# Sparse attention ahead of two dense layers: two tile groups per unit in place of three, a new order of steps, shorter lags and two early products

## The chip, the cores and the metric

The kernel runs on one core of one Trainium2 chip. The metric is the device time of one execution in microseconds (us). Engines are named as in the profile: PE is TensorE's matmul and PEld its weight load, DVE is VectorE, ACT is ScalarE, POOL is GpSimd, SP is SyncE, which issues the DMAs here.

## What is computed

```python
def _attn_ref(q, k, v):                       # B, H, S, D = 4, 8, 576, 64
    scores = scale * np.matmul(q, k.transpose(0, 1, 3, 2))
    mask_local = (rel >= 0) & (rel < 32)                     # heads 0 to 3
    mask_strided = (rel >= 0) & (pos[None, :] % 32 == pos[:, None] % 32)   # heads 4 to 7
    scores = np.where(masks, scores, -1e9)
    attn = softmax(scores)
    return np.matmul(attn, v)
...
x = attn_out.transpose(0, 2, 1, 3).reshape(2304, 512)
h = x @ w_in;  x = (h * np.cos(h)) @ w_out                   # 512 -> 2048 -> 512
g = x @ w_gate;  x = (g * sigmoid(g) * (x @ w_val)) @ w_out2   # 512 -> 1536 -> 512
```

The dense layers' weights come as 64-bit numbers in memory and are converted on the chip.

## The kernel before, in words

Attention works on 16 units (a batch and a pair of heads). Eight are local, with 9 tiles of 64 queries against 96 keys, and eight are strided, with 11 subtiles of 54 positions. Units go in pairs, one strided beside one local. `groups` (L78) cuts a unit into three groups: 3, 3 and 3 local tiles, or 4, 4 and 3 strided ones. The list `gs` (L780) has 48 groups, strided and local by turns, and the loop at L818 makes one step for each group and eight more to drain.

A group passes through several engines, one stage at a time, and `LAGS` says how many steps after its scores each stage is issued:

- `scores` (L460): PE multiplies q by k for each tile and head in 32-bit floats, into one PSUM bank. One matmul from `hot` (L472) fills the bank's columns that the tiles leave over, and one (L473) adds the mask. Together these two always cover 512 columns or nearly so.
- `top` (L475): DVE takes the row maxima of all the group's tiles in one instruction (L478).
- `exps` (L480), one step later: ACT, one instruction per tile (L484), into a buffer `e_l` or `e_s`.
- `sums` and `norm`, two steps later: DVE's row sums (L493) and reciprocals (L496), and POOL's multiplication (L498).
- `transposes` (L500), 5 steps later: PE. `evac` (L510): ACT copies the result out of PSUM (L515).
- `values` (L517), 6 steps later: PE multiplies by v (L526). `put` (L530), 7 steps later: ACT writes the result into `xy`, the dense layers' input.

All queues are filled in program order, with no scheduler, so an instruction that waits holds back everything behind it on its engine. Beside the groups, each step from number `KP` on calls `pump`, which takes work from a list `fill` until `PUMP` credits are spent. Here the list holds the preparation of `w_in`: for each of its 16 slices a maximum (L257) and two DVE steps of conversion (L261, L265), later a scaled high half on ACT (L275) and its low half on DVE (L278, called a lo here). Beside these stand maxima of the slices of `w_out` (L204, a scan here). One credit stands for about one microsecond of DVE.

The weight slices arrive through six buffers `raw`, each 512 KB: a scan or a conversion frees one and issues the next load. Loads of `w_out` are held back until step `RELEASE`.

After the last group's scores the loop drains. It starts the first of the dense layer's products there: `up1` (L604) for slice m = 0 is 12 matmuls of 512 columns, issued in two halves, `EARLY` being the number of such products. In other steps without scores `keep_warm` (L814) issues one small matmul. Then come 5 blocks of tokens with 16 slots each: a slot is one `up1`, a chain of ACT and DVE steps on its result (L617, L620, L624, L627), and pumped work. In block 0 the slots hold no second-layer matmuls. An `up1` needs a PSUM buffer: one of four `bank` tiles, or in some odd slots of block 0 an `acc` tile. A `bank` comes free when L627 has read it.

Of the kernel before, what the change touches and what calls it, by code (L numbers as in the profile page):

```python
# [20 lines left out]
STRIDE = 32  # L21
# [29 lines left out]
LAGS = (2, 5, 6, 7)  # L51
WARM = 11
PUMP, KP = 1.05, 8
XSAT = 12
EARLY, K0 = 1, 1
# [4 lines left out]
RELEASE = 30  # L60
# [17 lines left out]
def groups(p):  # L78
    return [(0, 3), (3, 3), (6, 3)] if is_local(p) else [(0, 4), (4, 4), (8, 3)]


def build(tc, qk_l, qk_s, v_l, v_s, w_in, w_out, w_gate, w_val, w_out2, fixed, out):
    nc = tc.nc
    wide = w_in.dtype != F32
    with ExitStack() as ctx:
# [322 lines left out]
        words = [128, 2 * LW, 2 * SW]  # L408
        fix = ap.tile([128, sum(words)], F32, name="fix", bufs=1)
        id32, ml, ms = (fix[:, sum(words[:i]):sum(words[:i + 1])] for i in range(3))  # L410
        ml, ms = (t.bitcast(BF16).rearrange("p (n w) -> p n w", n=4) for t in (ml, ms))
        e_s = [ap.tile([128, 2, 64, 2], F32, name=f"e_s{i}", bufs=1) for i in range(4)]
        e_l = [ap.tile([128, 3, LW + 1], F32, name=f"e_l{i}", bufs=1) for i in range(4)]
# [38 lines left out]
        class Group:  # L452
# [7 lines left out]
            def scores(self):  # L460
# [3 lines left out]
                mask = (ml[:, 0:3] if self.g == 0 else ml[:, 1:4]) if self.loc else ms[:, 0:n]  # L464
# [7 lines left out]
                nc.tensor.matmul(out=b[:, 288:512], lhsT=ones16, rhs=hot[:, 0:224], start=False, stop=False)  # L472
                nc.tensor.matmul(out=self.sc, lhsT=id16, rhs=mask, start=False, stop=True)  # L473

            def top(self):  # L475
                self.mx = ap.tile([128, 4], F32, name="mx", bufs=3)
                m = self.mx[:, 0:self.n]
                nc.vector.tensor_reduce(out=m, in_=self.sc, op=ALU.max, axis=AX.X, negate=True)  # L478

            def exps(self):  # L480
                self.t = (e_l if self.loc else e_s)[(self.i // 2 * 3 + self.g) % 4]
# [4 lines left out]
            def sums(self):  # L486

                self.ls = ap.tile([128, 4], F32, name="ls", bufs=5)
                if self.loc:
                    self.l, self.e = self.ls[:, 0:3], self.t  # L490
# [9 lines left out]
            def transposes(self):  # L500
                if self.loc:
                    self.tp = pa.tile([128, self.n, 128], F32, name="tp")[0:LW]
                    for i in range(self.n):
                        nc.tensor.transpose(self.tp[:, i, :], self.t[:, i, 0:LW], id32)
                else:
                    self.tp = pa.tile([128, 2, 128], F32, name="tp")
                    for i in range(2):
                        nc.tensor.transpose(self.tp[:, i, :], self.t[:, i].rearrange("p k u -> p (k u)"), id32)

            def evac(self):  # L510
                if self.loc:
                    self.pt = ap.tile([LW, 3, 128], F32, name="pt", bufs=2)
                else:
                    self.pt = ap.tile([128, 2, 128], F32, name="pts", bufs=2)
# [857 lines left out]
```

## Time and profile before

| | |
|---|---|
| median of 3 runs | 860.14 us (859.79 to 863.77) |
| the profiled execution: time, and its span | 859.9 us, 858.0 us |
| busy share of the span | PE 98%, PEld 70%, DVE 76%, ACT 61%, POOL 23% |
| last scores of attention, first unbroken run of dense matmuls | about 91 us, 101.8 us |
| granted TensorE clock | 0.999 of full speed |

Matmuls are pipelined, so a PE that counts as busy need not be at its peak; the distance from one start to the next tells what an instruction costs its engine. The last 750 us are dense products that PE streams almost without a break.

### The profile page before, as it was taken

The numbers are of one execution on the slowest core, as the hardware profiler recorded it, in microseconds if no ns is written. First come the engines' busy times: TensorE is split into PE (matmuls) and PEld (weight loads), VectorE is DVE, ScalarE is ACT, GpSimd is POOL, SyncE is SP. The second block draws the span as 40 slices with busy tenths as digits, with TensorE's granted clock in tenths as the row PEclk, the third lists the DMA queues.
The fourth block names the chain that finished last, engine by engine and source line by source line (L and its number), as shares of the span: only waits on it lengthen the run. The fifth ranks groups of instructions, "written<-read, shape, count | busy, mean of one in ns | idle before, by whom it ended". The sixth has DMA issues, their size and how long they took to land.

```text
span 858.0 us, 18371 instructions
## 1 busy us (share of the span) xinstructions
PE 844.6 (98%) x7223; PEld 601.7 (70%) x7223; DVE 653.0 (76%) x1256; ACT 519.4 (61%) x1047; POOL 197.8 (23%) x249
## 2 busy tenths in 40 slices
PE   9999999999999999999999999999999999999998
PEld 5776544444444444555666788888888899999998
DVE  6999989997888978788996378567756765765562
ACT  6898889554657766768885466545344444444440
POOL 4444234211445546423223100000000000000000
PEclk9999999999999999999999999999999999999999
DMA  9998832897567566515356257667776788789894
GB/s 364 408 359 283 276 105 74 278 343 261 165 201 244 193 215 205 177 34 179 129 194 249 71 196 282 230 217 261 239 261 232 244 274 288 277 310 321 321 321 143
DMA packets 53605, 202.21 MB, mean 236 GB/s; under 512 B 5264, under 2 KB 15888, under 8 KB 49680
## 3 DMA queue, kind: packets, MB, share of 16 engines
q1 hardware_dynamic: 53520, 201.06, 67.1%
q8 instruction: 56, 0.92, 0.4%
q14 instruction: 29, 0.24, 0.1%
HBM read 177.05 MB, written 23.99 MB: 234 GB/s over the span
## 4 chain that ended last, share of the span: by engine, by line
PE 85%; DVE 11%; ACT 2%; issue 1%; POOL 0%; POOLq 0%; ACTq 0%; DVEq 0%
PE acc L737 14%; PE bank L584 14%; PE bank L586 14%; PE bank L585 14%; PE acc L584 9%; PE acc L586 9%; PE acc L585 9%; PE bank L470 1%; DVE ls L493 1%; DVE pw_in L257 1%; DVE xs L278 1%; DVE mx L478 1%; DVE wi L261 1%; DVE wi L265 1%; DVE tb L620 1%
## 5 line engine op out<-in xcount | busy, mean ns | idle before, releaser
L584 PE MATMUL bank<-xs,wi 128*128 128x256 f16 (+3 forms) x776 | 231.1, 298 | 4.4 <-DVE q L145 1.7
L586 PE MATMUL bank<-xs,wi 128*128 128x256 f16 (+3 forms) x776 | 231.1, 298 | 0.0
L585 PE MATMUL bank<-xs,wi 128*128 128x256 f16 (+3 forms) x776 | 231.1, 298 | 0.0
L632 POOL TENSOR_TENSOR arena<-tb,arena 128x512 f16<-128x512 f32 (+1 forms) x80 | 91.7, 1147 | 238.4 <-ACT arena L631 216.3
L585 PEld LDWEIGHTS <-wi 128*128 128x128 f16 x880 | 86.1, 98 | 41.4 <-issue 7.2
L584 PE MATMUL acc<-arena 128*128 128x512 f16 (+1 forms) x320 | 114.5, 358 | 0.0
L585 PE MATMUL acc<-arena 128*128 128x512 f16 (+1 forms) x320 | 114.5, 358 | 0.0
L586 PE MATMUL acc<-arena 128*128 128x512 f16 (+1 forms) x320 | 114.5, 358 | 0.0
L584 PEld LDWEIGHTS <-wi 128*128 128x128 f16 x880 | 86.1, 98 | 36.1 <-issue 1.1
L586 PEld LDWEIGHTS <-wi 128*128 128x128 f16 x880 | 86.1, 98 | 34.8
L737 PEld LDWEIGHTS <-arena 128*128 128x128 f16 x1080 | 100.7, 98 | 8.1
L722 POOL TENSOR_TENSOR wi<-tb 128x256 f32<-128x256 f32 (+1 forms) x30 | 20.2, 673 | 338.6 <-DVE tb L704 338.6
L707 ACT ACTIVATE arena<-tb 128x256 f16<-128x256 f32 (+3 forms) x59 | 28.6, 485 | 98.7 <-DVE tb L704 90.3
L1235 DVE TENSOR_TENSOR arena<-bank,cv 128x512 f32<-128x512 f32 (+1 forms) x60 | 37.9, 636 | 66.0 <-PE bank L586 65.3
L737 PE MATMUL acc<-arena 128*128 128x256 f16 (+1 forms) x702 | 82.0, 265 | 0.0
L586 PEld LDWEIGHTS <-arena 128*128 128x128 f16 x600 | 58.7, 98 | 32.8
L584 PEld LDWEIGHTS <-arena 128*128 128x128 f16 x600 | 58.7, 98 | 32.6
L585 PEld LDWEIGHTS <-arena 128*128 128x128 f16 x600 | 58.7, 98 | 32.6
L631 ACT ACTIVATE arena<-tb 128x512 f16<-128x512 f32 (+1 forms) x80 | 46.6, 582 | 52.8 <-PE acc L586 51.2
L617 ACT ACTIVATE tb<-bank,quarter,c 128x512 int32<-128x512 f32 (+1 forms) x74 | 53.6, 724 | 34.4 <-PE bank L586 26.9
L704 DVE SCALAR_TENSOR_TENSOR tb<-tb,c,arena 128x512 f32<-128x512 f32 (+1 forms) x60 | 41.7, 694 | 35.8 <-ACT tb L699 35.8
L1231 ACT ACTIVATE cv<-bank 128x512 f32<-128x512 f32 (+1 forms) x90 | 49.2, 547 | 30.1 <-PE bank L586 29.1
(144 smaller groups left out, 1717.2 us busy)
## 6 DMA issues: line engine op xcount, KB each, us to landing
wi<-w SPq DMA_DIRECT2D x20, 1792.0 KB, 7.8
arena<-w SPq DMA_DIRECT2D x60, 576.0 KB, 4.8
raw<-w_out SPq DMA_DIRECT2D x56, 512.0 KB, 4.9
arena<-w SPq DMA_DIRECT2D x10, 1792.0 KB, 8.0
raw<-w_gate SPq DMA_DIRECT2D x24, 512.0 KB, 4.1
raw<-w_val SPq DMA_DIRECT2D x24, 512.0 KB, 5.9
w<-arena SPq DMA_DIRECT2D x42, 256.0 KB, 3.1
raw<-w_in SPq DMA_DIRECT2D x16, 512.0 KB, 9.1
```

The lines of the kernel that those rows point to most:

```text
L584: nc.tensor.matmul(out=o, lhsT=w[:, 0, c], rhs=x[0], start=first, stop=False, **kw)
L585: nc.tensor.matmul(out=o, lhsT=w[:, 0, c], rhs=x[1], start=False, stop=False, **kw)
L586: nc.tensor.matmul(out=o, lhsT=w[:, 1, c], rhs=x[0], start=False, stop=last, **kw)
L617: nc.scalar.activation(out=c["w"].bitcast(I32), in_=c["ph"], func=AF.Identity, scale=turn[c["blk"]], bias=quarter)
L631: nc.scalar.activation(out=g[:, 0, 0:n], in_=w, func=AF.Copy)
L632: nc.gpsimd.tensor_tensor(out=g[:, 1, 0:n], in0=w, in1=g[:, 0, 0:n], op=ALU.subtract)
L704: nc.vector.scalar_tensor_tensor(out=t, in0=t, scalar=s_g[c["blk"]], in1=c["C"][m][:, 1, 0:c["n"]], op0=ALU.mult, op1=ALU.mult)
L707: nc.scalar.activation(out=to, in_=src, func=AF.Copy, scale=2.0 ** -11)
L722: nc.gpsimd.tensor_tensor(out=t_sums[:, 0, 0:h], in0=c["t"][0][:, h:2 * h], in1=c["t"][0][:, 0:h], op=ALU.subtract)
L737: nc.tensor.matmul(out=o[:, c], lhsT=w[:, 256 * i + 128 * c:256 * i + 128 * c + 128], rhs=unit(u)[:, x:x + h], start=j == c == i == 0, sto ...
L1231: nc.scalar.activation(out=t, in_=src, func=AF.Copy)
L1235: nc.vector.tensor_tensor(out=c["C"][m][:, :, h * right:h * right + h], in0=p, in1=t, op=ALU.add)
```

## The change

A unit is cut into two groups, of 5 and 4 local tiles or 6 and 5 strided ones, so there are 32 groups and steps (`ROUND` = 4 per pair of units). The order within a step is new: `norm` directly follows `sums`, PE's transposes stand behind the scores, ACT's `exps` ahead of its `evac`, and DVE's `top` between two halves of the pumped work. The lags become 2, 3, 4 and 5. The tiles `e_l` and `e_s` are larger, three of each. A group of five local tiles transposes into two PSUM tiles of the pool's two. Pumping starts at step 6 with 1.55 credits a step and 2.2 in the drain. Two `up1` are issued in the drain. The condition added in the last hunk changes nothing, since slots 0 and 1 are both issued in the drain now. The scans of `w_out` are attached one slice later, with the same count, and the table of masks is laid out for five local tiles and one strided one.

```diff
-LAGS = (2, 5, 6, 7)
+LAGS = (2, 3, 4, 5)
+ROUND = 4
-PUMP, KP = 1.05, 8
+PUMP, PUMP_END, KP = 1.55, 2.2, 6
-EARLY, K0 = 1, 1
+EARLY, K0 = 2, 1
-RELEASE = 30
+RELEASE = 18
 def groups(p):
-    return [(0, 3), (3, 3), (6, 3)] if is_local(p) else [(0, 4), (4, 4), (8, 3)]
+    return [(0, 5), (5, 4)] if is_local(p) else [(0, 6), (6, 5)]
...
-        e_s = [ap.tile([128, 2, 64, 2], F32, name=f"e_s{i}", bufs=1) for i in range(4)]
-        e_l = [ap.tile([128, 3, LW + 1], F32, name=f"e_l{i}", bufs=1) for i in range(4)]
+        e_s = [ap.tile([128, 3, 64, 2], F32, name=f"e_s{i}", bufs=1) for i in range(3)]
+        e_l = [ap.tile([128, 5, LW + 1], F32, name=f"e_l{i}", bufs=1) for i in range(3)]
...
-                nc.tensor.matmul(out=b[:, 288:512], lhsT=ones16, rhs=hot[:, 0:224], start=False, stop=False)
+                nc.tensor.matmul(out=b[:, n * w:512], lhsT=ones16, rhs=hot[:, 0:512 - n * w], start=False, stop=False)
...
+                for a, z in ((0, 3), (3, 5)) if self.loc and self.n > 4 else ((0, self.n if self.loc else 3),):
+                    t = pa.tile([128, 4, 128], F32, name="tp")[0:LW if self.loc else 128, 0:z - a]
...
             if group(LAGS[0]):
                 group(LAGS[0]).sums()
-            if group(LAGS[1]):
-                group(LAGS[1]).transposes()
+                group(LAGS[0]).norm()
             if group(0):
                 group(0).scores()
-                group(0).top()
...
                     up1(0, m, range(KC // 2, KC), early)
-                    up1_a(early)
-                    steps.append((0, m, early))
             elif not group(0):
                 keep_warm()
+            if group(LAGS[1]):
+                group(LAGS[1]).transposes()
             if group(LAGS[3]):
                 group(LAGS[3]).put()
+            if group(1):
+                group(1).exps()
             if group(LAGS[1]):
                 group(LAGS[1]).evac()
             if group(LAGS[2]):
                 group(LAGS[2]).values()
...
+            if 0 <= begun < 2 * EARLY and begun % 2:
+                up1_a(early)
+                if steps:
+                    up1_b(steps[-1][2])
+                    up1_c(steps[-1][2])
+                if len(steps) > 1:
+                    up1_d(steps[-2][2])
+                steps.append((0, begun // 2, early))
+            share = 0 if k < KP else PUMP if group(0) else PUMP_END
+            pump(share * 0.5)
+            if group(0):
+                group(0).top()
...
+            pump(share * 0.5)
```

DVE, in the middle of attention, while `w_in` is converted. Names: `mx` are maxima, `ls` sums, `e_l` and `e_s` the local and strided exponentials. Before:

```order
L257 TENSOR_REDUCE pw_in<-raw 128x1
L261 TENSOR_SCALAR wi<-wi 128x512
L496 RECIPROCAL ls<-ls 128x3
L493 TENSOR_REDUCE ls<-e_s_98 128x4
L478 TENSOR_REDUCE mx<-bank 128x4
L265 SCALAR_TENSOR_TENSOR wi<-raw,wi 128x512
L257 TENSOR_REDUCE pw_in<-raw 128x1
L496 RECIPROCAL ls<-ls 128x4
L493 TENSOR_REDUCE ls<-e_l_102 128x3
L478 TENSOR_REDUCE mx<-bank 128x3
```

The same place in the changed program:

```order
L258 TENSOR_REDUCE pw_in<-raw 128x1
L479 TENSOR_REDUCE mx<-bank 128x6
L262 TENSOR_SCALAR wi<-wi 128x512
L266 SCALAR_TENSOR_TENSOR wi<-raw,wi 128x512
L494 TENSOR_REDUCE ls<-e_l_103 128x4
L497 RECIPROCAL ls<-ls 128x4
L258 TENSOR_REDUCE pw_in<-raw 128x1
L479 TENSOR_REDUCE mx<-bank 128x5
L262 TENSOR_SCALAR wi<-wi 128x512
L266 SCALAR_TENSOR_TENSOR wi<-raw,wi 128x512
```

Three instructions of a group now stand against three of conversion, where they stood against two, and the reciprocal follows its sums with no pumped work between.

PE, one step with local scores, before (`tp` is the transposes' PSUM tile, `po` that of the values):

```order
L470 MATMUL bank<-qkl 64x96 x6
L472 LDWEIGHTS ones_77
L472 MATMUL bank<-hot,ones_77 128x224
L473 LDWEIGHTS id_76
L473 MATMUL bank<-fix,id_76 128x288
L526 MATMUL po<-pt,vl 64x64 x6
L504 MATMUL tp<-fix,e_l_102 96x128 x3
```

And in the changed program:

```order
L471 MATMUL bank<-qkl 64x96 x10
L473 LDWEIGHTS ones_77
L473 MATMUL bank<-hot,ones_77 128x32
L474 LDWEIGHTS id_76
L474 MATMUL bank<-fix,id_76 128x480
L507 MATMUL tp<-fix,e_s_99 128x128 x3
L527 MATMUL po<-pt,vl 64x64 x10
```

The filling and mask matmuls cover the same 512 columns once for five tiles instead of three, and the transposes come between the mask and the values.

DVE, from the last group's maxima (first row here) into the drain, in the changed program (`pw_out` is a scan, `wi<-wi` a lo):

```order
L479 TENSOR_REDUCE mx<-bank 128x4
L205 TENSOR_REDUCE pw_out<-raw 128x1
L494 TENSOR_REDUCE ls<-e_s_98 128x6
L497 RECIPROCAL ls<-ls 128x6
L279 SCALAR_TENSOR_TENSOR wi<-wi,s_1510 128x512
L205 TENSOR_REDUCE pw_out<-raw 128x1
L279 SCALAR_TENSOR_TENSOR wi<-wi,s_1510 128x512
L205 TENSOR_REDUCE pw_out<-raw 128x1
L494 TENSOR_REDUCE ls<-e_l_101 128x4
L497 RECIPROCAL ls<-ls 128x4
L152 TENSOR_SCALAR c_1763<-inv_1145,inv_1511 128x1
L279 SCALAR_TENSOR_TENSOR wi<-wi,s_1510 128x512
```

The last group's sums stand behind three scans and two lo. After the last row shown, a scan and four more pairs of lo and scan follow before the first L621 (L620 before), which works on the product m = 0.

## Rows read from the trace of the kernel before

**Rows 1.** Stretches: us, busy us (instructions) by engine, clock, DMA share, GB/s.

```profile
20.00:40.00 20.00, 19.78 (x332) 14.09 (x330) 19.86 (x52) 17.31 (x66) 9.80 (x15) 1.00 1.03 407
92.00:102.00 10.00, 9.13 (x112) 5.46 (x110) 9.51 (x20) 9.22 (x28) 1.93 (x4) 1.00 0.87 268
102.00:120.00 18.00, 18.00 (x85) 8.20 (x84) 16.39 (x30) 13.97 (x21) 4.57 (x5) 1.00 0.57 187
120.00:140.00 20.00, 20.00 (x96) 9.11 (x95) 17.45 (x35) 18.21 (x30) 8.84 (x8) 1.00 0.15 53
```

**Rows 2.** Timeline of DVE in attention: start us, duration us, instruction.

```profile
50.50 0.17 DVE L496 RECIPROCAL ls<-ls 128x4 f32<-128x4 f32 x1
50.58 0.42 DVE L493 TENSOR_REDUCE ls<-e_l 128x3 f32<-128x291 f32 x1
50.92 0.45 DVE L478 TENSOR_REDUCE mx<-bank 128x3 f32<-128x288 f32 x1
51.29 0.41 DVE L261 TENSOR_SCALAR wi<-wi 128x512 int32<-128x512 int32 x1
...
52.43 0.35 DVE L493 TENSOR_REDUCE ls<-e_s 128x4 f32<-128x220 f32 x1
52.70 0.37 DVE L478 TENSOR_REDUCE mx<-bank 128x4 f32<-128x216 f32 x1
52.99 0.68 DVE L562 TENSOR_REDUCE parts<-xy 128x1 f32<-128x512 f32 x1
...
90.34 0.31 DVE L478 TENSOR_REDUCE mx<-bank 128x3 f32<-128x162 f32 x1
90.57 0.67 DVE L204 TENSOR_REDUCE pw_out<-raw 128x1 f32<-128x512 f32 x1
```

**Rows 3.** Timeline of PE in attention: a four-tile strided step, a three-tile one.

```profile
50.23 0.67 PE L470 MATMUL bank<-qks 64*64 64x54 f32 x16
51.13 0.68 PE L526 MATMUL po<-pts,v_pair 108*64 108x54 f32 x16
51.74 0.44 PE L508 MATMUL tp<-fix,e_s 128*128 128x128 f32 x2
52.11 0.71 PE L470 MATMUL bank<-qkl 64*64 64x96 f32 x12
...
88.51 0.56 PE L470 MATMUL bank<-qks 64*64 64x54 f32 x12
90.13 0.71 PE L470 MATMUL bank<-qkl 64*64 64x96 f32 x12
```

**Rows 4.** Chain that ended last: the first pumped DVE instruction (start, us, what).

```profile
17.88 0.59 DVE pw_in L257
```

**Rows 5.** Waits of ACT, 17 to 91 us: us in total, times, longest.

```profile
ACT wi L254 <- DMA raw<-w_in: 2.5, 2, 2.3
```

**Rows 6.** Timeline of DVE and PE from the last maxima into the dense layer.

```profile
91.69 0.45 DVE L478 TENSOR_REDUCE mx<-bank 128x3 f32<-128x288 f32 x1
...
101.37 0.68 DVE L204 TENSOR_REDUCE pw_out<-raw 128x1 f32<-128x512 f32 x1
101.78 0.38 PE L584 MATMUL acc<-xs,wi 128*128 128x512 f16 x1 [0.49 <-ACT xy L539]
101.97 0.74 DVE L278 SCALAR_TENSOR_TENSOR wi<-wi,s 128x512 f16<-128x512 f32 x1
101.99 0.38 PE L585 MATMUL acc<-xs,wi 128*128 128x512 f16 x1
...
103.88 0.75 DVE L620 SCALAR_TENSOR_TENSOR tb<-bank,c,tb 128x512 f32<-128x512 f32 x1
```

**Rows 7.** Groups by line and form, 0 to 102 us: busy us, mean ns, idle before.

```profile
L498 POOL TENSOR_TENSOR e_l<-e_l,ls 128x288 f32<-128x288 f32 x24 | 16.0, 666 | 23.9 <-DVE ls L496 11.7 <-PE tp L508 3.0 <-ACT e_l L484 2.7
L515 ACT ACTIVATE pt<-tp 96x384 f32<-96x384 f32 x24 | 12.4, 517 | 1.5 <-PE tp L504 1.2
```

**Rows 8.** Timeline of PE, end of block 0: its wait at slot 16.

```profile
142.01 0.38 PE L584 MATMUL bank<-xs,wi 128*128 128x512 f16 x1 [1.11 <-DVE tb L627]
```

More of the change, by code (lines that the diff above doesn't have):

```diff
@@ L777, in quarter_out @@
                 store("12", 0, h)
-        gs = [Group(i + d, g) for i in range(0, len(units), 2) for g in range(3) for d in range(2)]
+        gs = [Group(i + d, g) for i in range(0, len(units), 2) for g in range(2) for d in range(2)]
         load_qk(0)
@@ L807, in build @@
         scale_later(TW_IN, "in")
-        split_chain([("in", j, wi) for j in range(M1)], 2, lambda j: scan_later("out", j + 1) if j + 1 < M1 else top_later("out"))
+        split_chain([("in", j, wi) for j in range(M1)], 2, lambda j: scan_later("out", j - M1 + 16) if j > M1 - 16 else None)
+        for j in range(16, M1):
+            scan_later("out", j)
+        top_later("out")
         for i in range(2):
@@ L848, in build @@
                 group(LAGS[2]).values()
-            if group(0) and g == 5:
-                for j in (i + 2, i + 3):
-                    if i and j < len(units):
-                        load_v(j)
-                for j in (i + 6, i + 7):
-                    if j < len(units):
-                        load_qk(j)
-            if group(1):
-                group(1).exps()
-            pump(PUMP if k >= KP else 0)
-            if group(LAGS[0]):
-                group(LAGS[0]).norm()
+            if 0 <= begun < 2 * EARLY and begun % 2:
[10 more added lines that the diff above has]
+                group(0).top()
+                if g in (1, 2) and i + g + 1 < len(units):
+                    scale_q(i + g + 1)
+                if g == ROUND - 1:
+                    for j in (i + 2, i + 3):
+                        if i and j < len(units):
+                            load_v(j)
+                    for j in (i + 6, i + 7):
+                        if j < len(units):
+                            load_qk(j)
+            pump(share * 0.5)
             if k >= RELEASE:
@@ L1072, in build @@
                     urge(scale_pieces([1, 2, 3], sy, 2))
-                c = up1(blk, m, spare=slot // 2 % KC if slot % 2 and slot < HEAD - 4 else None)
+                c = up1(blk, m, spare=slot // 2 % KC if slot % 2 and 1 < slot < HEAD - 4 else None)
                 if blk == NBLK - 1 and m in (7, 14):
```

44 lines of the change are left out of this document (20 added, 24 removed).

## The prediction

> **What bounds the kernel now.** I read the stretches first. From 20 us on PE and DVE are both busy nearly all the time, ACT a little less, and the granted clock is 1.00 throughout [rows 1]. From 102 us PE streams dense products; the change does not touch those, so what counts is when that stream starts and what interrupts it. A busy PE proves little, so I read distances between starts from the timelines. On DVE one instruction follows the other without a gap [rows 2]; in attention it is full. PE's steps follow without a gap too [rows 3]. The pumped work was dosed so that both are full, and a saving on one alone would leave the other in place. Pumped work starts at 17.88 [rows 4], and ACT had waited 2.3 us for the first slice of `w_in` before that [rows 5]; this landing sets the start in both kernels. The last group's maxima start on DVE at 91.69, the stream of products (m = 1) at 101.78 [rows 6]. In between lies the drain of 10.1 us, with one product in it. After that PE waits 1.11 us at slot 16, for a `bank` that DVE's L627 has not yet read [rows 8].
>
> **Attention on DVE.** From start to start [rows 2], maxima cost 0.37, 0.29 and 0.23 us for 288, 216 and 162 elements: 0.0011 us an element and 0.05 fixed. Sums cost 0.34 and 0.27 for 291 and 220: 0.001 an element, 0.05 fixed. A reciprocal costs 0.08. A pair of units (six steps) takes 2 x 0.29 + 0.23 + 3 x 0.37 = 1.92 for maxima, 3 x 0.34 + 3 x 0.27 = 1.83 for sums and 0.48 for reciprocals: 4.23 us. In four steps, maxima of 324, 270, 480 and 384 elements cost 0.41 + 0.35 + 0.58 + 0.47 = 1.81, sums of 330 twice, 485 and 388 cost 0.38 + 0.38 + 0.53 + 0.43 = 1.72, and reciprocals 0.32: 3.85 us. The elements are the same; what goes is the fixed part of two groups.
>
> From 17.88 to 91.69 are 73.8 us. In them DVE handles 39 groups, 6.5 pairs, for 27.5 us, so 46.3 us remain for 39 pumps of 1.05, 41 credits: 1.13 us a credit, waits included. In the changed order DVE handles 25 groups (6.25 pairs, 24.1 us) between its first pumped instruction and the last maxima, and 25.5 pumps of 1.55, 39.5 credits, at 1.13 us: 44.6. That is 68.7 us, so the last maxima start at 86.6, **5.1 us earlier**. Of this 3.4 us are work that is gone or was counted in more pairs; 1.7 us are credits handed to the drain.
>
> [...]
>
> **PE and ACT there.** A four-tile strided step takes PE 1.88 us (50.23 to 52.11) and a three-tile one 1.62 (88.51 to 90.13) [rows 3], 0.26 a tile. Six and five tiles take 1.88 + 0.52 and 1.88 + 0.26, and 0.1 more each for a third transpose, where two took 0.37: 4.74 us for a strided unit against 2 x 1.88 + 1.62 = 5.38. I take the same 0.6 us for a local unit: 1.2 us a pair, against DVE's 0.38 and its share of credits. So PE gets slack, and DVE alone binds. ACT keeps its `exps`, one per tile, has one `evac` fewer per strided unit and fewer `put`, and had 2.7 us of slack in 20 [rows 1]; I cost it at nothing, covered by DVE, and if that cover goes it is next to bind, with about 0.2 us a pair saved. POOL, half idle [rows 1], multiplies the same elements in fewer instructions.
>
> **The drain.** The time of the last maxima, 86.6, is called T. DVE issues those (0.47), a scan, the sums and reciprocal of the group before (0.46), two lo and two scans, and the last sums and reciprocal (0.51). A scan is 0.60 from start to start (101.37 to 101.97) and a lo 0.65 [rows 6], so this ends at T + 4.5. POOL's multiplication of 288 elements takes 0.67 [rows 7]; 384 take at most 0.9: T + 5.4. PE has meanwhile done a warming matmul, two groups' transposes, two groups' values and the product m = 0, about 5.5 us after its last scores, so it hardly waits. Then come four transposes (0.55), values of 20 matmuls (16 take 0.61 [rows 3], so 0.75), half of m = 1, the last values (0.61), the other half, and a warming matmul (0.2). A product is 12 matmuls of 0.215 us (101.78 to 101.99 [rows 6]), 2.58 us. Sum 4.7, so m = 2 can start at T + 10.1 = 96.7. Before, m = 2 followed 2.58 us after 101.78, at 104.36. At that point the changed kernel is **7.7 us ahead**: 5.1 from attention and 2.6 from a second product inside a drain of the same length.
>
> **What is late next.** In the drain DVE now has 13.2 credits in six steps, against 8.4 in eight. By the order, its first L620 comes five pairs of lo and scan after the last sums: T + 4.5 + 5 x 1.25 + 0.2 = 97.5, 0.8 us after m = 2 has started, where it was 0.5 us ahead (103.88 against 104.36 [rows 6]). DVE is thus 1.3 us later relative to PE. Up to the L627 that frees the `bank` for slot 16 the order also gives it one more conversion of a `w_out` slice (L261, L265, L278: 0.45 + 0.60 + 0.65 = 1.7 us). That makes 3.0 us. Against it stand 4.2 us that DVE was idle from 102 to 140 [rows 1], for ACT and for products not yet done. If all of that absorbs it, PE's wait stays at about 1.1 us; if none does, it grows by 3.0. I take the middle, **1.5 us lost**.
>
> **Sum**: 859.9 - 7.7 + 1.5 = 853.7 us for the profiled execution. The median of the runs shown is 0.2 higher, so I forecast 853.9. About 0.5%, 4.3 us, is what a measurement of this kernel can tell from no change.
>
> **Rivals.**
> (a) DVE's total decides. Then what PE gains it gives back waiting for `bank` tiles. None of the idle time is recovered (3.0 instead of 1.5), and in the drain the scans are held up: one 512 KB slice per 1.25 us is 420 GB/s, and the loads never showed more than 407 [rows 1]. Ten slices past the six buffers' start, with ACT's high halves in the same queue as `exps` and `evac`, I price at 2.5 us. 859.9 - 7.7 + 3.0 + 2.5 = 857.7, with the 0.2, 857.9. For it: DVE is 87 to 99% busy from 20 to 140 us [rows 1]. Against it: PE found what it needed until slot 16. Chance 0.20.
> (b) The loads bind the first half. At 407 GB/s and a share of 1.03 [rows 1] DMA is full until about 55 us. If attention cannot go faster while that lasts, half of the 5.1 us is lost: 856.5. Against it: the waits for loads are a few at the start [rows 5], so buffers run ahead. Chance 0.10.
> (c) Slower. Five local tiles take both `tp` buffers, and the group after them finds none until ACT has evacuated the first. ACT's `evac` stands behind `put` and `exps`; if PE has to wait for a whole evacuation (0.52 us [rows 7]) and 0.8 us of `exps` ahead of it, twice a pair, that is 2.6 us on a PE that saved 1.2: 1.4 x 6.5 pairs = 9 us longer than before, against 2.6 gained in the drain, about 866. It decides from waits of about 0.8 us each. Against it: so far ACT waits for transposes (1.2 us in all [rows 7]) and not PE for ACT. Chance 0.10.
> (d) The clock. [...] Chance 0.04. [...]
>
> **How the numbers follow.** My forecast has 0.56, the likeliest, with a range of its own from 851 to 856. The 80% range must take in (a), (b) and (d) above, and below a drain that is 1.5 us shorter and a DVE that recovers all its idle time: 850.0 to 859.0. Outside lie (c) and the outer edges. Faster by over 0.5% means under 855.8: nearly all of the forecast, a third of (b) and a little of (a), 0.60. Within: most of (a), the rest of (b), and (d), 0.29. Slower 0.11, from (c) and a drain that fails.
>
> **What would show it.** Right: 32 groups of maxima on DVE at 0.35 to 0.6 us from start to start; their last at about 86.6 us; PE with visible gaps in attention, DVE with few; m = 2 at about 97; a wait of PE before slot 16 of 1 to 4 us on L628. Wrong: PE waiting for `evac` in attention; maxima ending after 89 us with DVE idle; the product m = 2 after 99 us; or several waits on `bank` in block 0 that sum to more than 5 us.

## The result: slower by 0.8%, and the profile after

The changed kernel takes 867.98 us in the median of 12 executions (864.65 to 870.39), the kernel before 860.66 (12 executions, 859.79 to 863.77): a ratio of 1.0078, 95% interval 1.006 to 1.0095. The forecast was 853.9. Four executions lie at 864.65 to 864.9, with a mean granted clock of 0.998; eight at 867.67 to 870.39, with 0.988 to 0.994; the kernel before is at 0.999. The profiled execution is one of the four: 864.9 us, span 863.1, against 859.9 and 858.0. So 5.0 us are in the profile, and at the median some 3 us more go with the clock.

From here on, lines of the changed file count: in the attention and behind it they are one higher than before (L478 is L479, L584 is L585).

The stretches of the changed kernel, in the columns of [rows 1]:

```profile
20.00:40.00 20.00, 16.73 (x316) 13.00 (x312) 19.47 (x40) 17.86 (x64) 7.12 (x9) 1.00 1.02 407
70.00:80.00 10.00, 9.02 (x141) 7.48 (x141) 9.75 (x25) 8.63 (x33) 5.43 (x6) 0.83 0.40 131
92.00:102.00 10.00, 8.65 (x111) 5.32 (x107) 9.73 (x20) 9.22 (x25) 3.63 (x3) 1.00 0.78 252
102.00:120.00 18.00, 15.66 (x87) 7.27 (x86) 16.52 (x33) 14.86 (x25) 3.02 (x4) 1.00 0.78 275
120.00:140.00 20.00, 20.00 (x95) 9.08 (x94) 19.44 (x34) 17.08 (x28) 8.97 (x8) 1.00 0.16 53
```

PE has the slack that was predicted (16.73 of 20 us where it had 19.78), VectorE (DVE) is still full, and from 70 to 80 us the granted clock is 0.83. The same stretch of the kernel before:

```profile
70.00:80.00 10.00, 10.00 (x170) 7.18 (x169) 9.47 (x31) 7.71 (x31) 4.32 (x7) 1.00 0.77 234
```

The timeline of DVE in the changed kernel (start, duration, instruction); of the two steps of conversion, L262 is called the shift from here on and L266 the merge:

```profile
50.79 0.55 DVE L494 TENSOR_REDUCE ls<-e_l 128x4 f32<-128x388 f32 x1
51.37 0.18 DVE L497 RECIPROCAL ls<-ls 128x4 f32<-128x4 f32 x1
51.46 0.66 DVE L266 SCALAR_TENSOR_TENSOR wi<-raw,wi 128x512 int32<-128x512 int32 x1
...
53.67 0.48 DVE L494 TENSOR_REDUCE ls<-e_s 128x6 f32<-128x330 f32 x1
54.19 0.19 DVE L497 RECIPROCAL ls<-ls 128x6 f32<-128x6 f32 x1
54.29 0.65 DVE L266 SCALAR_TENSOR_TENSOR wi<-raw,wi 128x512 int32<-128x512 int32 x1
...
92.94 0.55 DVE L479 TENSOR_REDUCE mx<-bank 128x4 f32<-128x384 f32 x1
93.41 0.67 DVE L205 TENSOR_REDUCE pw_out<-raw 128x1 f32<-128x512 f32 x1
```

From start to start, sums of 388 elements take 0.58 us and sums of 330 take 0.52; 0.43 and 0.38 were predicted. The reciprocal, which reads them, now stands right behind. The last maxima start at 92.94, not at 86.6, and later than before (91.69 [rows 6]).

The timeline of PE, at the places where it pauses or could be compared. `tops` and `q` belong to the scale of a weight: DVE writes `tops` (L139), PE multiplies it (L145), and DVE takes a maximum `q` of the product (L146).

```profile
49.64 1.04 PE L471 MATMUL bank<-qkl 64*64 64x96 f32 x20
50.61 0.19 PE L473 MATMUL bank<-hot,ones 128*128 128x32 bf16 x1
...
70.98 0.75 PE L507 MATMUL tp<-fix,e_l 128*96 128x128 f32 x5 [2.43 <-POOL e_l L499]
71.66 1.18 PE L527 MATMUL po<-pts,v_pair 108*64 108x54 f32 x24
72.77 1.86 PE L471 MATMUL bank<-qkl 64*64 64x96 f32 x20
74.57 0.21 PE L473 MATMUL bank<-hot,ones 128*128 128x32 bf16 x1
...
104.40 0.38 PE L585 MATMUL bank<-xs,wi 128*128 128x512 f16 x1
...
114.67 0.22 PE L145 MATMUL bank<-tops,ones 128*128 128x128 bf16 x1 [2.34 <-DVE tops L139]
...
144.44 0.38 PE L585 MATMUL bank<-xs,wi 128*128 128x512 f16 x1 [1.00 <-DVE tb L628]
...
219.81 0.38 PE L585 MATMUL bank<-xs,wi 128*128 128x512 f16 x1 [0.51 <-DVE q L146]
...
367.18 0.32 PE L585 MATMUL bank<-xs,wi 128*128 128x384 f16 x1 [2.72 <-DVE q L146]
...
402.88 0.32 PE L585 MATMUL bank<-xs,wi 128*128 128x384 f16 x1 [0.38 <-DVE q L146]
```

The product m = 2 starts at 104.40, as before (104.36), so nothing is left of the 7.7 us. Slot 16 comes at 144.44, 2.43 us after [rows 8]; the pause of 2.34 us ahead of 114.67, in front of the scale of `w_out`, makes nearly all of this. A wait of 2.72 us at 367.18 was one of 0.71 before:

```profile
365.84 0.32 PE L584 MATMUL bank<-xs,wi 128*128 128x384 f16 x1 [0.71 <-DVE q L145]
...
397.63 0.32 PE L584 MATMUL bank<-xs,wi 128*128 128x384 f16 x1 [0.38 <-DVE q L145]
```

From there on everything is 5.25 us late (402.88 against 397.63), and the end 5.1. The pause of 2.43 us ahead of 70.98 is followed by a granted clock of 0.50 from 72.4 to 75.0 us: the same 20 matmuls take 1.80 us from start to start at 72.77 and 0.97 at 49.64.

For the runs below, the distances between starts on DVE, less idle time, are added up from the first pumped instruction to the start of the last maxima (us). Group work is maxima, sums and reciprocals; pumped work is the rest. The first pumped instruction doesn't start at the same time in all of them, so the length tells what attention costs.

| kernel | first pumped at | group work | pumped work | idle | length | last maxima at |
|---|---|---|---|---|---|---|
| before | 17.80 | 27.8 | 44.4 | 1.7 | 73.9 | 91.69 |
| changed | 17.66 | 28.3 | 42.7 | 4.2 | 75.3 | 92.94 |
| reciprocal later | 17.42 | 24.8 | 48.2 | 7.3 | 80.3 | 97.72 |
| the same, no product | 16.35 | 24.7 | 40.1 | 6.0 | 70.7 | 87.08 |
| regrouping alone, old order | 15.83 | 24.0 | 43.5 | 1.5 | 69.1 | 84.88 |
| the same, lags 2, 4, 5, 6 | 18.26 | 25.5 | 42.0 | 3.8 | 71.3 | 89.56 |

### The profile page after: what moved, and what is told of

Its sections match the earlier page's. It is cut to its first block, busy times and chain, and to the rows that moved or that the text cites. A ratio compares the mean times of both kernels' runs of the same rounds, so it can differ in the third digit from the quotient of the medians.

```text
span 863.1 us, 18093 instructions
## 1 busy us (share of the span) xinstructions
PE 834.5 (97%) x7187; PEld 599.6 (69%) x7187; DVE 654.1 (76%) x1208; ACT 518.0 (60%) x1019; POOL 199.2 (23%) x230
## 4 chain that ended last, share of the span: by engine, by line
PE 81%; DVE 9%; ACT 6%; issue 1%; POOL 1%; DMA 1%; ACTq 0%; POOLq 0%; DVEq 0%
PE acc L738 14%; PE bank L585 13%; PE bank L587 13%; PE bank L586 13%; PE acc L587 8%; PE acc L586 8%; PE acc L585 8%; ACT e_l L485 1%; DVE mx L479 1%; DVE ls L494 1%; DVE xs L279 1%; ACT tb L618 1%; POOL arena L633 1%; DMA raw<-w_in 1%; DVE pw_in L258 1%
## 5 line engine op out<-in xcount | busy, mean ns | idle before, releaser
L585 PE MATMUL bank<-xs,wi 128*128 128x256 f16 (+3 forms) x780 | 232.6, 298 | 6.8 <-DVE q L146 4.3
L585 PE MATMUL acc<-arena 128*128 128x512 f16 (+1 forms) x320 | 114.5, 358 | 0.0
L585 PEld LDWEIGHTS <-wi 128*128 128x128 f16 x880 | 86.1, 98 | 38.5 <-issue 3.6
L585 PEld LDWEIGHTS <-arena 128*128 128x128 f16 x600 | 58.7, 98 | 32.6
```

The lines of the kernel that those rows point to most:

```text
L585: nc.tensor.matmul(out=o, lhsT=w[:, 0, c], rhs=x[0], start=first, stop=False, **kw)
```

## The experiments

### The reciprocal behind its sums, and the product beside the pumped work

```diff
             if group(LAGS[0]):
                 group(LAGS[0]).sums()
-                group(LAGS[0]).norm()
...
             pump(share * 0.5)
+            if group(LAGS[0]):
+                group(LAGS[0]).norm()
             if group(0):
                 group(0).top()
```

> The changed kernel with one edit: a step's reciprocal and GpSimd's product go behind the first half of the pumped work, so that another VectorE instruction stands between the sums and the reciprocal that reads them. Theory A (VectorE binds the attention, and a reciprocal right behind its sums costs about 0.14 us of latency each): the 25 sums between the first pumped instruction and the last maxima shrink from 14.5 us to about 11, the last maxima start near 89.5 instead of 92.94, and the time falls by 3 to 4 us, to about 864. Theory B (the short lags bind: engines wait for each other): GpSimd's product comes 1 to 2 us later with the transposes still one step behind, TensorE's wait for it grows over its 12 us, and the time stays at 868 or rises.

Measured: 871.24 us, ratio 1.0119 (1.0104 to 1.0134). The sums shrink as theory A says, to 0.405, 0.57 and 0.47 us, and group work falls by 3.5 us. But the pumped work grows by 5.5 and the idle time by 3.1, and the last maxima are later still. DVE and, behind it, POOL in this run:

```profile
50.05 1.09 DVE L262 TENSOR_SCALAR wi<-wi 128x512 int32<-128x512 int32 x1
51.06 0.48 DVE L494 TENSOR_REDUCE ls<-e_s 128x6 f32<-128x330 f32 x1
51.47 0.68 DVE L266 SCALAR_TENSOR_TENSOR wi<-raw,wi 128x512 int32<-128x512 int32 x1
...
49.87 0.99 POOL L499 TENSOR_TENSOR e_l<-e_l,ls 128x480 f32<-128x480 f32 x1 [1.97 <-DVE ls L497]
```

The shift L262 beside POOL's product takes 1.09 us; without a POOL instruction beside them, seven shifts take 0.42 on average. So I left the product out of the same kernel; its probabilities stay undivided.

```diff
                 nc.vector.reciprocal(out=self.l, in_=self.l)
                 e = self.e[..., 0:self.w]
-                nc.gpsimd.tensor_tensor(out=e, in0=e, in1=self.l.unsqueeze(len(e.shape) - 1).to_broadcast(list(e.shape)), op=ALU.mult)
```

> The changed kernel with the reciprocal behind the first half of the pumped work, as in the first experiment, and GpSimd's product of the attention left out: its probabilities stay undivided, all other instructions are there. Theory G (what the later reciprocal saved went into shift and merge, because GpSimd's product ran beside them): shifts take 0.35 us start to start and merges 0.61 where no scaling of queries runs beside them, the pumped work up to the last maxima falls from 48.2 us by 5 to 6.5 us, and the last maxima start 6 to 8 us earlier than in that run (97.72), at 90 to 92 or earlier. Rival: shifts and merges stay near 0.67 and 0.86 us, so something else slows them; last maxima later than 95.

Measured (one execution, 858.33 us): the pumped work falls by 8.1 us; the last maxima start at 87.08, 10.6 us earlier, of which 1.1 are an earlier first pumped instruction; slot 16 is at 137.90 (before: 142.01). The shift and its neighbour there:

```profile
46.52 0.41 DVE L262 TENSOR_SCALAR wi<-wi 128x512 int32<-128x512 int32 x1
46.85 0.54 DVE L494 TENSOR_REDUCE ls<-e_l 128x4 f32<-128x388 f32 x1
```

Theory G holds, with more than the 5 to 6.5 us that it expected. In the kernel before, the product runs mostly beside the next sums and maxima, and the maxima keep their time: 17 of 288 elements that run beside it for at least 95% of their time take the 0.37 us of [rows 2]. With the later reciprocal only a short maximum lies between it and the next shift or merge. So the product is running when these start, and what the sums save is paid there. In the changed kernel a pumped instruction follows the reciprocal at once: of those that met the product alone, three merges and four shifts that started before it keep 0.65 to 0.66 and 0.39 to 0.40 us, while one merge and four shifts that started while it ran took 1.12 and 0.50 to 0.94. The changed kernel itself pays no more of this than the one before: 42.7 us for 39.5 credits, and 44.4 for 41, are 1.08 us a credit in both.

### Longer lags

```diff
-LAGS = (2, 3, 4, 5)
+LAGS = (2, 4, 5, 6)
```

> The changed kernel with one edit: lags 2, 4, 5, 6 in place of 2, 3, 4, 5, so that transposes stand two steps behind the product that they read. Theory A (VectorE's work binds): TensorE's 12 us of waits for GpSimd's product go, but VectorE's group work stays at 28.3 us, the last maxima stay within 1.5 us of 92.94 and the time within 2 us of 868. Theory B (waits of the short lags bind): with those waits VectorE's 4.25 us of idle time go as well, the last maxima start before 90 and the time is 864 or less.

> Both edits on the changed kernel: reciprocal and product behind the first half of the pumped work, and lags 2, 4, 5, 6. Theory A: like the later reciprocal alone, near 864, with TensorE's waits gone at no further gain. Theory B: like the longer lags alone. If both hold, they add: 860 or less, last maxima near 87.

Measured: 869.89 (ratio 1.0114, 1.0097 to 1.013) and 872.89 (1.0142, 1.0127 to 1.0157). With lags alone, PE's waits for the product fall from 11.7 to 1.4 us between 20 and 100 us; PE then waits for ACT's copies and DVE's `tops`, 11.9 us in all where it was 12.2. DVE's account stays at 28.3 group work and 4.2 idle, as theory A says. The last maxima start at 90.99, 1.95 us earlier, because the first pumped instruction starts 2.1 us earlier (15.57). Theory B falls: the waits for the product cost PE, which has slack, and not the attention. With both edits DVE's account is that of the later reciprocal (24.7 group work, 48.3 pumped).

The rise comes behind attention, where PE reaches two scales sooner than DVE. The wait for that of `w_out` grows from 2.34 to 5.52 us, the one near 216 us from 0.70 to 4.13, and around both the clock falls (0.57 from 214 to 222 us); against that the wait near 367 us is 2.3 us shorter. Stretches of the run with longer lags:

```profile
100.00:110.00 10.00, 4.80 (x35) 2.12 (x33) 8.73 (x16) 8.78 (x16) 0.00 (x0) 0.93 0.89 315
110.00:120.00 10.00, 9.68 (x35) 3.99 (x36) 8.29 (x18) 5.03 (x9) 1.16 (x1) 0.73 0.66 223
```

### The regrouping alone, in the old order of a step

The kernel before with two groups for three and what belongs to it; the old order of a step, the old lags, one first product in the tail.

```diff
+ROUND = 4
-PUMP, KP = 1.05, 8
+PUMP, KP = 1.55, 6
-RELEASE = 30
+RELEASE = 18
...
-    return [(0, 3), (3, 3), (6, 3)] if is_local(p) else [(0, 4), (4, 4), (8, 3)]
+    return [(0, 5), (5, 4)] if is_local(p) else [(0, 6), (6, 5)]
```

> The kernel before with the regrouping alone: two groups for three, tiles and masks to fit, the pumped share scaled by 48/32 to 1.55 (with 6 in place of 8 steps before the first one, 18 in place of 30 before free buffers are released), and the old order of a step, the old lags 2, 5, 6, 7, one first product in the tail and the old place of the scans. Theory A: the maxima stand between sums and reciprocal here, so the sums take 0.38, 0.53 and 0.43 us and VectorE's group work is about 24.5 us; the last maxima start at 87 to 89, and the time is 854 to 858, faster than before. Theory B (the coarser group itself makes engines wait, by its two transposed tiles of local groups): last maxima at 92 or later, 862 or more. Theory C (the loss comes from the tail and from the queue's order behind it, not from attention): 857 to 861 whatever the last maxima do.

Measured: 904.29, ratio 1.0512 (1.049 to 1.0534). This edit changed the computation: with four steps to a round and lag 6, a strided pair's values were loaded into a tile whose old values the group before had still to read, so those groups multiply with other values, and PE waited 36.1 us for `v_pair`. It says nothing on the theories. The loads went behind the reading:

```diff
-            if group(0) and g == ROUND - 1:
-                for j in (i + 2, i + 3):
-                    if i and j < len(units):
-                        load_v(j)
+            if g == 1:
+                for j in (i, i + 1):
+                    if i > 2 and j < len(units):
+                        load_v(j)
```

> The kernel before with the regrouping alone, as in the run before, with the loads of the values moved from a round's last step to the second step of the next one, behind the values that still read the same tile. Theory D (VectorE's own time binds up to slot 16, and it is set by where GpSimd's product falls: beside sums and maxima it slows nothing, beside shift, merge and low halves it makes each 0.3 to 0.5 us longer): the sums take 0.405, 0.57 and 0.465 us, shifts and merges stay near 0.52 and 0.70 us, the last maxima start at 87 to 89 and the time is 854 to 858. Theory B (coarse groups make engines wait): last maxima at 92 or later with VectorE idle for 5 us or more, time 861 or more.

Measured: 860.75, ratio 1.0012 (1.0 to 1.0024). DVE in attention, and two places of PE, in this run:

```profile
51.28 0.17 DVE L497 RECIPROCAL ls<-ls 128x6 f32<-128x6 f32 x1
51.38 0.61 DVE L494 TENSOR_REDUCE ls<-e_l 128x5 f32<-128x485 f32 x1
51.91 0.54 DVE L479 TENSOR_REDUCE mx<-bank 128x4 f32<-128x384 f32 x1
52.38 1.26 DVE L563 TENSOR_REDUCE parts<-xy 128x1 f32<-128x512 f32 x2
...
84.88 0.55 DVE L479 TENSOR_REDUCE mx<-bank 128x4 f32<-128x384 f32 x1
...
99.25 0.38 PE L585 MATMUL acc<-xs,wi 128*128 128x512 f16 x1 [0.66 <-ACT xy L540]
...
139.41 0.38 PE L585 MATMUL bank<-xs,wi 128*128 128x512 f16 x1 [1.04 <-DVE tb L628]
...
362.15 0.32 PE L585 MATMUL bank<-xs,wi 128*128 128x384 f16 x1 [2.72 <-DVE q L146]
```

Attention does what the prediction said: sums of 485 at 0.53, group work 24.0 us, and 69.1 us from the first pumped instruction to the last maxima, 4.8 less than before. These start at 84.88, 6.8 us earlier; the other 2.0 us come from the first pumped instruction, which has seven maxima ahead of it in place of nine and starts at 15.83. The stream (m = 1) starts at 99.25, 2.5 us earlier: the tail has eight steps in both, but pumps 1.55 in place of 1.05 credits in each, 4 credits more, at 1.08 us 4.3. Slot 16 is 2.6 us earlier. That gain is gone again behind it, 2.0 us with the wait of 2.72 at 362, which is in the changed kernel too, and 0.6 with one of 0.51 near 214.8. The profiled span is 858.2 against 858.0, and the time misses theory D's 854 to 858.

> The same with the lags 2, 4, 5, 6 and one step less in the tail. Theory D: VectorE's work as in the run with lags 2, 5, 6, 7; the drain is some 1.5 us shorter, the time 0 to 1.5 us below that run's. Theory B: shorter lags bring waits back, TensorE's for GpSimd's product and ScalarE's copies sum to over 6 us, and the time is 2 us or more above it.

> The same with two first products in the tail. If the second product in the tail is a gain by itself, TensorE works in a part of the drain where it waited, and the time falls by 1 to 2.5 us. If VectorE binds to slot 16, TensorE waits later for the same VectorE work (for tops or for tb), and the time stays within 0.7 us.

Measured: 864.44 (ratio 1.0048, 1.0032 to 1.0065) and 859.84 (0.9997, 0.9988 to 1.0006). With shorter lags the waits for the product are back (10.2 us in all up to 150 us, 1.3 with the old lags), idle time and sums grow, and the first pumped instruction starts 2.4 us later; here theory B has a point. The second product in the tail takes 4.6 us off, but not where it was expected: the matmul that waits 0.65 us for `q` near 208 us starts at 208.55 without it and 208.16 with it. The rest is a wait of 2.98 us for `tb` at 365, with a granted clock of 0.50 from 365 to 368 us, where the kernel with it has a wait of 0.71 for `q` and no fall of the clock.

```diff
-EARLY, K0 = 2, 1
+EARLY, K0 = 1, 1
...
-                c = up1(blk, m, spare=slot // 2 % KC if slot % 2 and 1 < slot < HEAD - 4 else None)
+                c = up1(blk, m, spare=slot // 2 % KC if slot % 2 and slot < HEAD - 4 else None)
```

> The changed kernel with one edit: one first product in the tail, as before. If VectorE binds to slot 16, the time stays within 1 us of 868 and the wait of TensorE for tops (2.34 us) shrinks by what the first product is later. If the second product in the tail is what hurts (it puts TensorE ahead of VectorE), the wait for tops goes and the time falls by 2 us or more; if it helps, the time rises by 1 to 2.5 us.

Measured: 863.44, ratio 1.0041 (1.0026 to 1.0056), 4.5 us below the changed kernel. The wait for `tops` near 114 us is gone, yet slot 16 stands at 144.56 against 144.44: VectorE binds up to there, and the second product is worth 0.1 us. The time falls by more than 2 us, as the rival said, but not for its reason: the profiled span is 2.1 us shorter, since the wait near 367 us is 0.28 here, and the rest goes with the clock (0.992 to 0.998).

### The scale near 365 us

This place is 200 us behind anything the diff touches. DVE in the regrouping alone, and behind it in the kernel of the last run below, where L624 and L631 are the lines L621 and L628:

```profile
359.42 0.75 DVE L599 TENSOR_SCALAR xy<-acc,c 128x512 f32<-128x512 f32 x1 [0.54 <-PE acc L587]
360.08 0.61 DVE L621 SCALAR_TENSOR_TENSOR tb<-bank,c,tb 128x384 f32<-128x384 f32 x1
360.61 1.29 DVE L279 SCALAR_TENSOR_TENSOR xs<-xy,s,xs 128x384 f16<-128x384 f32 x1
361.82 0.28 DVE L146 TENSOR_REDUCE q<-bank 128x1 f32<-128x128 f32 x1
```

```profile
360.40 0.75 DVE L602 TENSOR_SCALAR xy<-acc,c 128x512 f32<-128x512 f32 x1 [0.54 <-PE acc L590]
361.07 0.61 DVE L624 SCALAR_TENSOR_TENSOR tb<-bank,c,tb 128x384 f32<-128x384 f32 x1
361.60 1.29 DVE L279 SCALAR_TENSOR_TENSOR xs<-xy,s,xs 128x384 f16<-128x384 f32 x1
362.81 0.54 DVE L631 SCALAR_TENSOR_TENSOR tb<-tb,bank 128x384 f32<-128x384 f32 x1
...
364.17 0.61 DVE L279 SCALAR_TENSOR_TENSOR xs<-xy,s,xs 128x384 f16<-128x384 f32 x1
364.70 0.28 DVE L146 TENSOR_REDUCE q<-bank 128x1 f32<-128x128 f32 x1
```

L146 is the scale of the last weight; PE needs its `bank`. In the first it stands one product earlier in the program, behind stores that wait for a block's last matmuls, so its `bank` stays taken. The queue of pumped work is dosed by credits and has empty steps of 1.0 ahead of this scale; more of them move it back.

```diff
-                for i in range(3):
+                for i in range(5):
                     later(1.0, lambda: None)
```

> The changed kernel with one number altered far from the change: five empty steps instead of three in the queue of pumped work ahead of the last weight's scale, so that on VectorE the row L146 stands two products behind a finished block's two stores L599, as in the kernel before, and not right behind the first product. Theory E (the regrouped program fills its queue in another rhythm, and by that this scale falls where TensorE must wait for it): the wait of 2.72 us near 367 us falls to about 0.7 and the profiled span by 2 to 2.6 us, to about 860.5 to 861; the wait for tops near 114 us stays at 2.3 us and slot 16 at 144.4. Rival: the wait at 367 only covers VectorE's lateness and comes back behind it; the span stays at 863.

> The kernel before with the regrouping alone (old order of a step, lags 2, 5, 6, 7, loads of the values one round's second step later) and six empty steps for three ahead of the last weight's scale. Theory E: the wait of 2.72 us near 362 us falls to 0.7 or less; slot 16 stays at 139.4, and the time is 2 to 2.6 us below that of the regrouping alone, 857.5 to 859: faster than the kernel before by some 2 us. Rival: the 2.6 us gained at slot 16 are lost elsewhere and the time stays within 0.7 us of 860.7.

> The kernel before with the regrouping alone (old order of a step, lags 2, 5, 6, 7) and the last weight's scale set, by empty steps of 5.5 in all in place of 3, at the same place of VectorE's order as before: behind the second product's low half and ahead of its L628. Theory E: the wait near 364 us is 0.7, the next ones as before; of the 2.1 to 2.6 us gained at slot 16 some 2 stay, and the time is 857.5 to 858.5. Rival: as with six empty steps, 858.9, since VectorE's lateness comes back in other waits.

> The same with two first products in the tail and five empty steps, the row L146 in the same place. If VectorE alone sets slot 16, the time is that of the run with one first product, within 0.7 us. If TensorE's waits of the drain count, it falls by a further 1 to 2 us, to 856 or 857.

Measured: the changed kernel with five empty steps 863.78, ratio 1.0038 (1.0025 to 1.0051): the wait is 0.71, and the way from the wait at 211.33 to the one at 401.81 is 2.0 us shorter than the changed kernel's from 210.40 to 402.88. The profiled span falls by 1.1 us only, to 862.0, because a fall of the clock behind 115 us, shown below, makes slot 16 come 0.9 us later. The regrouping with six 858.93, ratio 0.9986 (0.9977 to 0.9995), faster than before; slot 16 at 139.90, a wait of 0.97 for `tb` left at 364.80. With 5.5 it is 859.95, ratio 0.9993 (0.9981 to 1.0004): the wait is 0.70, but the executions run from 857.71 to 863.19, and of those the four at clock 1.00 are 857.71 to 858.38. Theory E holds. The clock takes the rest, and the profiled execution (862.02 us, clock 0.992) shows how: in three stretches of attention the granted clock is 0.79 to 0.84, for instance

```profile
50.00:60.00 10.00, 8.02 (x123) 6.10 (x124) 8.29 (x24) 7.27 (x28) 5.02 (x6) 0.79 1.02 408
```

and DVE waits 5.1 us for PE's scores, where it waits 0.2 in the regrouping alone at clock 1.00. The length from the first pumped instruction to the last maxima is 73.5 us there against 69.1.

With two first products 862.93, ratio 1.0029 (1.0017 to 1.0041), against both theories: PE waits 2.72 us for ACT's `pt` ahead of 102.08 and the granted clock from 102 to 108 us is 0.50. That is the clock of rival (d), in another kernel.

### The clock

```diff
-            t, p = bank()[:, 0:128 * n].rearrange("p (n c) -> p n c", n=n), brief("q", n)
+            b = bank()
+            t, p = b[:, 0:128 * n].rearrange("p (n c) -> p n c", n=n), brief("q", n)
+            for _ in range(fill):
+                nc.tensor.matmul(out=b, lhsT=wi[0][:, 0, 0:128], rhs=wi[0][:, 0], start=True, stop=True)
             nc.tensor.matmul(out=t, lhsT=ones16, rhs=d, start=True, stop=True)
```

Here `fill` is 10 for the scale of `w_out` and 0 for every other.

> The changed kernel with ten matmuls of 512 columns, on data that nothing reads further, put in TensorE's queue ahead of the matmul that waits 2.34 us for tops near 114 us. Theory F (TensorE's pause there is what lets the granted clock fall later in most executions, and so makes the upper of the changed kernel's two levels of time, 867.7 to 870.4 us at clock 0.988 to 0.994): the pause is filled, all executions come out near the lower level, 864.5 to 865.5, at clock 0.998. Rival: the clock falls because of the pauses in the attention; then most executions stay at 867.7 or more.

Measured: 865.5, six executions: three at 864.72 or 864.73, one at 866.26, two at 869.54 and 869.71 with clock 0.990. The pause at 114 us is filled, and the slot behind it doesn't move (144.30). The upper level stays in two or three of six, where it was eight of twelve: this pause is not its cause, or not alone. It may be one of several: the changed kernel with five empty steps is the same program up to there and has the same pause in its profiled execution, and there the granted clock behind it is 0.57:

```profile
114.65 0.22 PE L145 MATMUL bank<-tops,ones 128*128 128x128 bf16 x1 [2.34 <-DVE tops L139]
```

```profile
115.00:119.00 4.00, 4.00 (x13) 1.45 (x12) 3.97 (x11) 2.29 (x4) 1.19 (x2) 0.57 0.48 169
```

```diff
+                    for _ in range(0 if a else 3):
+                        nc.tensor.matmul(out=t.rearrange("p a n -> p (a n)"), lhsT=ones16, rhs=hot, start=True, stop=True)
                     for i in range(a, z):
```

> The changed kernel with three matmuls of 512 columns, on data that nothing reads, ahead of each group's transposes, where TensorE waits for GpSimd's product. Theory H (TensorE's pauses in the attention lower the granted clock): the clock stays at 1.00 in all stretches of the attention of the profiled execution, also from 70 to 80 us, and no execution is above 866 us; clocks of 0.998 or more. Rival: the upper level, 867 to 870 at clock 0.988 to 0.994, stays in half of the executions or more. The 4 to 5 us that VectorE's group work and idle time cost are there in both.

> The changed kernel with one matmul of 512 columns ahead of each group's transposes, in place of three. Theory H: fewer executions at clocks below 0.995 than 8 of 12, median 865 to 866.5, the least time 864.7 to 865.5. Rival: as many as without it, median 867.5 or more.

> The regrouping in the old order of steps with 5.5 empty steps, as in the run before, and one matmul of 512 columns, on data that nothing reads, ahead of each group's transposes. Theory H (the spread of 857.7 to 863.2 us is the granted clock's, lowered by TensorE's pauses in the attention): clocks of 0.998 or more in nearly all executions, their spread under 2 us, median 857.7 to 859. Rival: the matmuls stand on the path (32 of 0.21 us, 6.8 us if all did), the least time rises above 859.

Measured with three: 869.59, ratio 1.0111 (1.0098 to 1.0124). The clock is 1.00 in three executions of four and 0.998 in the fourth, also from 70 to 80 us:

```profile
70.00:80.00 10.00, 9.18 (x153) 6.70 (x151) 9.86 (x21) 9.65 (x35) 3.89 (x4) 1.00 0.49 162
```

The spread is 1.5 us where it was 5.7. But the matmuls cost time themselves: DVE's idle time doubles to 8.3 us, slot 16 is at 149.19. So half of theory H holds: with PE's pauses in the attention filled, the clock stayed in these four executions. On the same chip, in the same comparison, the regrouping with 5.5 empty steps and no such matmuls had clocks down to 0.990. With one matmul in the changed kernel 868.53, ratio 1.0086 (1.007 to 1.0101), four executions of five at clock 0.994: not enough. With one matmul in the regrouping in the old order, whose pauses are shorter (1.98 us at most in attention, against 2.43), 858.63 (858.34 to 858.99), ratio 0.9979 (0.997 to 0.9988): all eleven executions at 0.999 or 1.00, slot 16 at 140.40, the wait at 365.03 at 0.71. This kernel is faster than the kernel before, by 0.2%. The last two ran on one chip; the same kernel without the matmul ran on another, so its wider spread is not a strict comparison. The regrouping with six empty steps, which has the same attention and no such matmul, had clocks of 0.997 or more on a third chip, so it isn't shown that the matmul holds the clock here.

## Why the prediction was wrong

**Attention on DVE: 5.1 us earlier predicted, 1.25 later measured.** The term failed at one place, "sums of 330 twice, 485 and 388 cost 0.38 + 0.38 + 0.53 + 0.43". Those distances came from [rows 2], where maxima stand between the sums and their reciprocal. The change writes the reciprocal right behind, and the sums take 0.52, 0.68 and 0.58; 25 groups cost 28.3 us where 24.1 were forecast. The regrouping itself was priced rightly: in the old order its groups take 24.0 us, and the length is 69.1 us where 68.7 were forecast. The prediction read what was removed and not which neighbour each instruction has. The other 2.5 us are DVE's idle time, on the page as three waits for ACT of 1.9, 1.2 and 1.2 us; in the old order they are 0.6 and 0.6. That ACT's new order makes them was not tried by itself.

**"This landing sets the start in both kernels."** This was misread, without harm to the sum. ACT's wait for a landing in [rows 5] is not ahead of the first pumped instruction but 21 us behind it:

```profile
38.60 0.68 ACT L254 ACTIVATE wi<-raw 128x512 f32<-128x512 f32 x1 [2.27 <-DMA raw<-w_in]
```

In the changed kernel pumped work starts at 17.66, as predicted, but in the regrouping alone at 15.83, so no landing holds it there.

**POOL "multiplies the same elements in fewer instructions".** True, and costed at nothing, which holds between these two kernels. But shifts and merges that started while the product ran took longer (a shift up to 1.09 us, where it takes 0.42 alone), so the product decides where a reciprocal may go; the prediction did not see that.

**PE and ACT there.** Right: PE has slack, and its 11.7 us of waits for POOL's product cost DVE nothing. What was missed is that the granted clock fell there: in the profiled execution it was 0.50 from 72.4 to 75.0 us, behind the pause of 2.43 us. The range and the chances also count rival (d), a lower clock in the drain; no run shows that term for the changed kernel, whose granted clock from 92 to 120 us was 1.00 in the profile. Where the clock fell in the slower executions no profile shows; the median is about 3 us beyond the profiled one.

**The drain and the second product.** From the last maxima to m = 2 it takes 11.5 us, 1.4 more than the 10.1; before it was 12.7. So the drain gained 1.2 us up to that point, not 2.6, and even that did not last: "2.6 from a second product" was worth 0.1 us at slot 16 in one pair of kernels and 0.4 near 208 us in the other, since PE then waits for DVE. That is rival (a), DVE's total decides; it got the bound right and its time, 857.9, wrong, because it took over the 7.7 us. Two signs that the prediction named for being wrong came: the last maxima behind 89 us with DVE idle, and m = 2 behind 99 us.

**What is late next.** The wait at slot 16 did not grow (1.00 us). From m = 2 to slot 16 2.4 us were lost, not 1.5, and they showed as the 2.34 us in front of the scale of `w_out`, which the prediction did not look for.

**Behind slot 16.** The sum let 710 us pass without a change. Slot 16 was 2.4 us late, the end 5.25: 2.0 more come from the scale near 367 us, 0.5 from a wait at 219.81 that is not there before, 0.3 from smaller places. The order of DVE's instructions alone, without any run, shows L146 one product earlier. Against the 853.7 forecast for the profiled execution, then, attention was late by 6.3 us, the drain by 1.4, the way to slot 16 by 0.9 and the way behind it by 2.8; 0.2 came back at the end.

Rivals (b) and (c) did not happen: the loads ran at 407 GB/s to 40 us as before and neither ACT nor DVE waited for one in the attention, and PE did not wait for an evacuation of `tp` in the attention. Open remains what starts each fall of the clock in the executions that were not profiled.

## What to carry to other kernels

Price an instruction by its distance to the next one, and check whether the next one in the new order reads its result, and which other engine works beside it; the regrouping made the attention 4.8 us shorter, as computed, and the new order with its lags made it 6.2 us longer again. Where work is dosed by credits from one queue, a saving in one stage shifts every later meeting of that queue with the main stream, so look at the scales and stores hundreds of microseconds behind the change. Slack on PE is not always free: here the granted clock was 0.50 behind pauses of 2.43 and 2.72 us, and in an execution with stretches of attention at 0.79 to 0.84 DVE waited 5.1 us for PE's scores, where it waited 0.2 at 1.00. A small matmul in the pauses is cheap to try; here three of them a group went with a clock of 0.998 or more and cost more than they saved, and what a single one is worth stays open.

## What the runs showed of the hardware that was not expected

Sums followed by the reciprocal that reads them cost 0.11 to 0.15 us more here than sums followed by another instruction (0.52 against 0.38 to 0.405 us for 330 elements). Between independent neighbours this doesn't show; their fixed part was 0.05 us [rows 2].

A shift of 128x512 took 0.42 us alone and up to 1.09 when it started while GpSimd's product ran (in the run with the later reciprocal), while 17 maxima of 288 elements beside the product kept their 0.37 us in the kernel before. Shifts and merges that started before the product kept theirs, too (0.39 to 0.40 and 0.65 to 0.66 us in the changed kernel).

A granted clock of 0.50 followed pauses of 2.43 us (from 72.4 to 75.0 us, in the changed kernel) and 2.72 us (from 102 to 108, in the run with two first products). Around pauses of 1.68 to 1.98 us in the profiled execution of the regrouping with 5.5 empty steps it was 0.79 to 0.84 over 10 us. The pause of 2.34 us ahead of the scale of `w_out` was followed by a clock of 1.00 in the profiled execution of the changed kernel and of 0.57 in that with five empty steps. So the length of a pause alone doesn't tell whether the clock falls.
